# Two experts' maximum as one product with w1 - w2, and Q transposed by the DMA from batch 2 on

## The chip, the cores and the metric

The kernel runs on one core of one Trainium2 chip. The metric is device time in microseconds (us). The engines are named as in the profile: PE is TensorE, PEld its weight loads, DVE is VectorE, ACT is ScalarE, POOL is GpSimd, SP is SyncE. POOL and SP issue the DMAs here.

## What is computed

A linear attention in front of a layer with two experts, of which the larger value is taken element by element:

```python
k_proj = np.einsum('ks,bhsd->bhkd', E, k)          # 8 batches, 8 heads, 1024 tokens, 64 wide
v_proj = np.einsum('ks,bhsd->bhkd', F, v)          # E, F: 64 x 1024
scores = scale * np.matmul(q, k_proj.transpose(0, 1, 3, 2))
attn = softmax(scores)
attn_out = np.matmul(attn, v_proj)
x = attn_out.transpose(0, 2, 1, 3).reshape(8192, 512)
h1 = x @ w1                                        # 512 x 1024
h2 = x @ w2                                        # 512 x 1024
out = np.maximum(h1, h2) @ w_out                   # 1024 x 512
```

Inputs and output are float32; the products are taken in float16 with float32 sums.

## The kernel before

The main loop runs over the 8 batches of 1024 tokens. In it PE works through the expert layer of batch b, and between its blocks stand, one step at a time, the pieces of the attention of batch b + 1. The order is written out by hand: each engine runs its instructions in the order of the program.

`moe_blocks` gives 24 blocks for a batch, in two halves of 512 tokens (j). A half has 8 `up` blocks and then 4 `down` blocks. An `up` block makes 128 of the 1024 hidden columns: four products with w2 into one PSUM bank, four with w1 into another (L272), each 128x512; ACT copies the first bank to SBUF (h2, L279), and DVE takes the maximum of the second bank and that copy, as float16, into `gt` (L280). A `down` block makes the result for 128 tokens: eight products of `gt` with w_out (L288), an ACT copy (L295) and an output DMA on SP's queue (L296). So every block is eight products.

The attention steps of a batch are: `step_kv` (K and V projected with E and F, 16 products, L147), `step_kpt` (K's projection transposed by PE, L161), and for each of four head pairs p: `step_qt` (eight 128x128 transposes of Q on PE, L180, into a float16 PSUM bank; a DVE copy of it into `qt_sb`, L187), `step_sc` (scores, L197; exp on ACT, L205) and `step_da` (denominators and attention, L216; ln and exp(-ln) on ACT, L224 and L225; and, one block later, the product on DVE into `xt_sb`, L228). `xt_sb` is the transposed x that the `up` blocks read. `plan` says after which block each step stands: `step_kv` after block 4, `step_kpt` after 6, the first `step_qt` and `step_sc` after 7 and 8, the last `step_da` after 20.

Batch 0 has no earlier expert work to stand between. Its attention runs first, by itself (the prologue): `step_kv`, `step_kpt`, then for each pair the next pair's `step_qt` and `step_sc` and a `step_da_half` for the first 512 tokens (L242, L250, L251, L254). The second halves stand behind the first four blocks of batch 0.

PSUM has four banks of tag `mm` (products of the expert layer, projections, transposes) and two double banks of tag `att`. Loads go through POOL's queue and turn float32 into float16 on the way; `k_sb`, `v_sb` and `q_sb` have two buffers each, so a load for batch b + 3 waits until batch b + 1 has been read. POOL's order is: K, V, Q of batch 0, the weights in chunks of 256 columns (w2 and w1 in turn), w_out, then K, V, Q of each further batch.

Of the kernel before, what the change touches and what calls it, by code (L numbers as in the profile page):

```python
# [16 lines left out]
def kernel(  # L17
# [27 lines left out]
    const = ctx.enter_context(tc.tile_pool(name="const", bufs=1))  # L45
    kvq = ctx.enter_context(tc.tile_pool(name="kvq", bufs=2))
    proj = ctx.enter_context(tc.tile_pool(name="proj", bufs=2))
    soft = ctx.enter_context(tc.tile_pool(name="soft", bufs=2))
    stage = ctx.enter_context(tc.tile_pool(name="stage", bufs=4))
    xpool = ctx.enter_context(tc.tile_pool(name="xpool", bufs=2))  # L50
    gpool = ctx.enter_context(tc.tile_pool(name="gpool", bufs=2))
    hpool = ctx.enter_context(tc.tile_pool(name="hpool", bufs=3))
    opool = ctx.enter_context(tc.tile_pool(name="opool", bufs=4))
    ps = ctx.enter_context(tc.tile_pool(name="ps", bufs=1, space=bass.MemoryType.PSUM))

    def mm_bank(dtype=FP32):
        return ps.tile(
            [128, 512 if dtype == FP32 else 1024], dtype, tag="mm", bufs=4, name="mm_ps"
        )

    def att_banks():
# [7 lines left out]
            name=nc.get_next_instruction_name(),  # L69
# [24 lines left out]
    tiles = {0: alloc_kvq()}  # L94
# [22 lines left out]
    ident16 = const.tile([128, 128], FP16)  # L117
# [17 lines left out]
    def new_attn(t):  # L135
        t["kp"] = proj.tile([KP, H, D], FP16, tag="kp", name="kp_sb")
        t["vp"] = proj.tile([128, H, D], FP16, tag="vp", name="vp_sb")
        t["kpt"] = proj.tile([128, H, KP], FP16, tag="kpt", name="kpt_sb")
        t["xt"] = xpool.tile([128, NP2, 2, HALF], FP16, tag="xt", name="xt_sb")
        t["qt"] = {}  # L140
        t["ex"] = {}

    def step_kv(t):
# [32 lines left out]
    def step_qt(t, p):  # L176
        qt_ps = mm_bank(FP16)
        for e in range(2):
            for i in range(NI):
                nc.tensor.transpose(  # L180
                    out=qt_ps[:, (e * NI + i) * 128 : (e * NI + i + 1) * 128],
                    in_=t["q"][:, 2 * p + e, 2 * i : 2 * i + 2, :],
                    identity=ident16,
                )
        qt = soft.tile([128, 2, HALF], FP16, tag="qt", name="qt_sb")
        t["qt"][p] = qt
        nc.vector.tensor_copy(out=qt.rearrange("q e n -> q (e n)"), in_=qt_ps)  # L187

    def step_sc(t, p):
        sc_ps = att_banks()
        qt = t["qt"].pop(p)
        for o in range(2):
            for e in range(2):
                pos = D * (o ^ e)
                nc.tensor.matmul(  # L197
                    out=sc_ps[pos : pos + KP, e, :],
                    lhsT=t["kpt"][o * D : (o + 1) * D, 2 * p + e, :],
                    rhs=qt[o * D : (o + 1) * D, e, :],  # L200
                    start=True, stop=True,
                )
        ex = stage.tile([128, 2, HALF], FP16, tag="ex", name="ex_sb")
        t["ex"][p] = ex
        nc.scalar.activation(out=ex, in_=sc_ps, func=ACTF.Exp, scale=scale)  # L205
# [29 lines left out]
    def step_da_half(t, p, o):  # L235
        ex = t["ex"][p]
        da_ps = att_banks()
        for i in range(2):
            for e in range(2):
                r = o ^ e  # L240
                rows = slice(r * KP, (r + 1) * KP)
                nc.tensor.matmul(  # L242
                    out=da_ps[e * D : (e + 1) * D, i, :],
                    lhsT=t["vp"][rows, 2 * p + e, :] if i else ones16[rows, :],
                    rhs=ex[rows, e, :],
                    start=True, stop=True,
                )
        ld = soft.tile([128, HALF], FP32, tag="ldh", name="ldh_sb")
        rec = soft.tile([128, HALF], FP32, tag="rech", name="rech_sb")
        nc.scalar.activation(out=ld, in_=da_ps[:, 0, :], func=ACTF.Ln)  # L250
        nc.scalar.activation(out=rec, in_=ld, func=ACTF.Exp, scale=-1.0)  # L251

        def finish():
            nc.vector.tensor_tensor(  # L254
                out=t["xt"][:, p, o, :], in0=da_ps[:, 1, :], in1=rec, op=ALU.mult
            )

        return finish


    def moe_blocks(b, t):
        xt = t["xt"]
        for j in range(2):
            gt = gpool.tile([128, NFB, HALF], FP16, tag="gt", name="gt_sb")
            for fb in range(NFB):
                def up(fb=fb, j=j, gt=gt):
                    banks = []
                    for w_sb in (w2_sb, w1_sb):
                        h_ps = mm_bank()
                        banks.append(h_ps)  # L270
                        for r in range(NDC):
                            nc.tensor.matmul(  # L272
                                out=h_ps,
                                lhsT=w_sb[:, r, fb * 128 : (fb + 1) * 128],
                                rhs=xt[:, r, j, :],
                                start=(r == 0), stop=(r == NDC - 1),
                            )
                    h2 = hpool.tile([128, HALF], FP32, tag="h2", name="h2_sb")
                    nc.scalar.copy(out=h2, in_=banks[0])  # L279
                    nc.vector.tensor_tensor(  # L280
                        out=gt[:, fb, :], in0=banks[1], in1=h2, op=ALU.max
                    )
                yield up
            for i in range(NI):
                def down(i=i, j=j, gt=gt):
                    op_ps = mm_bank()
                    for fb in range(NFB):
                        nc.tensor.matmul(  # L288
                            out=op_ps,
                            lhsT=gt[:, fb, i * 128 : (i + 1) * 128],  # L290
                            rhs=wo_sb[:, fb, :],
                            start=(fb == 0), stop=(fb == NFB - 1),
                        )
                    o_sb = opool.tile([128, DM], FP32, tag="o", name="o_sb")
                    nc.scalar.copy(out=o_sb, in_=op_ps)  # L295
                    nc.sync.dma_start(  # L296
                        out=out.rearrange("(n p c) m -> n p c m", p=128, c=NC)[
                            b, :, 2 * i + j, :
                        ],
                        in_=o_sb,  # L300
                    )
                yield down


    t = tiles[0]
# [11 lines left out]
    first = {n: (step_da_half, n, 1) for n in range(NP2)}  # L317
    plan = {
        4: [(step_kv,)], 6: [(step_kpt,)], 7: [(step_qt, 0)], 8: [(step_sc, 0)],
        9: [(step_qt, 1)], 11: [(step_da, 0)], 12: [(step_sc, 1)], 13: [(step_qt, 2)],  # L320
        14: [(step_da, 1)], 15: [(step_sc, 2)], 16: [(step_qt, 3)], 17: [(step_da, 2)],
        18: [(step_sc, 3)], 20: [(step_da, 3)],
    }

    for b in range(B):
        nxt = None
        if b + 1 < B:
            nxt = tiles[b + 1] = alloc_kvq()
            for n, src in (("k", k), ("v", v), ("q", q)):
                load(nxt, n, src, b + 1, 0, H)  # L330
            new_attn(nxt)
        pending = None
        for n, block in enumerate(moe_blocks(b, tiles[b])):
            block()
            if pending is not None:
                pending()
                pending = None
            if b == 0 and n in first:
                s = first[n]
                pending = s[0](tiles[0], *s[1:])  # L340
            if nxt is None:
                continue
            for s in plan.get(n, ()):
                r = s[0](nxt, *s[1:])
                if r is not None:
                    pending = r
        del tiles[b]


# [28 lines left out]
```

## Time and profile before

| | us |
|---|---|
| median of 3 runs | 439.12 |
| lowest, highest | 438.16, 440.35 |
| the profiled execution | 439.34 |
| its span, first to last instruction | 437.6 |
| DVE busy, ACT busy in the span | 160.7, 215.4 |

The page gives, for each engine, its busy time as a share of the span; then a chain of work followed back from the last instruction, at each step to whatever released it; and groups of instructions by line, with the mean duration of one. A matmul's duration (382 ns in the group of L272) is longer than the distance from one to the next, since they are pipelined. The granted clock of PE is 1.000 over the span.

```profile
L272 PE MATMUL mm_ps<-xt_sb,w_sb 128*128 128x512 f16 x1024 | 237.2, 382 | 0.7 <-DVE xt_sb L254 0.7
L288 PE MATMUL mm_ps<-wo_sb,gt_sb 128*128 128x512 f16 x512 | 116.7, 379 | 0.0
```

The line of a group reads: line, engine, operation, written <- read, shape, count | busy us in total, mean ns of one | idle us of the engine before them, and what ended it.

### The profile page before, as it was taken

The page shows a single profiled execution, that of the slowest core. Times are in us where ns is not written, and L with a number is a line of the kernel's source. Part 1 is how long each engine was busy: PE and PEld are TensorE (multiplying, and loading weights), DVE is VectorE, ACT ScalarE, POOL GpSimd, SP SyncE. Part 2 cuts the span into 40 slices and gives each one's busy share as a digit, 9 for nine tenths or more (in the row PEclk, how much of TensorE's full clock was granted, in tenths as well). Part 3 has the DMA queues.
Part 4 walks back from the last instruction along what each step waited for, and adds up shares of the span by engine and source line. Part 5 has one row for each costly group of instructions (what it writes and reads, how often), then busy time and mean ns, then how long its engine had stood idle before and what let it go on. Part 6 is the DMA issues. An engine that isn't in the chain of part 4 may idle for free.

```text
span 437.6 us, 5860 instructions
## 1 busy us (share of the span) xinstructions
PE 413.1 (94%) x2352; PEld 180.3 (41%) x2352; DVE 160.7 (37%) x231; ACT 215.4 (49%) x322; POOL 31.8 (7%) x44
## 2 busy tenths in 40 slices
PE   2558999999999999999999999999999999999996
PEld 1232343444444444444443444444443444344442
DVE  0132543524163343524263243524254342434130
ACT  1145547643566346653466345743476336653332
POOL 6450100001000010001000010000000000000000
PEclk9999999999999999999999999999999999999999
DMA  9999999924907195532917177350100102020202
GB/s 163 202 198 207 207 212 242 155 97 61 228 6 140 49 144 145 80 114 29 220 41 128 66 120 170 55 140 1 72 25 25 73 0 97 0 79 19 97 0 96
DMA packets 39707, 45.99 MB, mean 105 GB/s; under 512 B 1664, under 2 KB 31360, under 8 KB 39680
## 3 DMA queue, kind: packets, MB, share of 16 engines
q0 software_dynamic: 30304, 28.31, 41.5%
q1 hardware_dynamic: 9376, 17.31, 10.7%
q8 instruction: 18, 0.29, 0.3%
q14 instruction: 9, 0.07, 0.1%
HBM read 57.15 MB, written 16.78 MB: 169 GB/s over the span
## 4 chain that ended last, share of the span: by engine, by line
PE 92%; DMA 3%; ACT 2%; DVE 1%; issue 1%; POOL 1%; POOLq 0%
PE mm_ps L272 52%; PE mm_ps L288 26%; PE mm_ps L147 4%; PE att_ps L216 4%; PE mm_ps L180 3%; PE att_ps L197 3%; DMA v_sb<-in_v_dram 3%; ACT ex_sb L205 1%; DVE qt_sb L187 1%; PE att_ps L242 1%; ACT rech_sb L251 1%; ACT ldh_sb L250 1%; PE mm_ps L161 0%; POOL k_sb L89 0%; DVE xt_sb L254 0%
## 5 line engine op out<-in xcount | busy, mean ns | idle before, releaser
L272 PE MATMUL mm_ps<-xt_sb,w_sb 128*128 128x512 f16 x1024 | 237.2, 382 | 0.7 <-DVE xt_sb L254 0.7
L280 DVE TENSOR_TENSOR gt_sb<-mm_ps,h_sb 128x512 f16<-128x512 f32 x128 | 88.3, 690 | 174.3 <-PE mm_ps L272 101.8
L272 PEld LDWEIGHTS <-w_sb 128*128 128x128 f16 x1024 | 94.9, 98 | 124.7 <-issue 21.2
L288 PE MATMUL mm_ps<-wo_sb,gt_sb 128*128 128x512 f16 x512 | 116.7, 379 | 0.0
L279 ACT COPY h_sb<-mm_ps 128x512 f32<-128x512 f32 x128 | 74.6, 583 | 79.6 <-PE mm_ps L272 79.6
L295 ACT COPY o_sb<-mm_ps 128x512 f32<-128x512 f32 x64 | 37.4, 584 | 80.6 <-PE mm_ps L288 80.6
L288 PEld LDWEIGHTS <-gt_sb 128*128 128x128 f16 x512 | 48.3, 98 | 58.3 <-issue 4.5
L228 DVE TENSOR_TENSOR xt_sb<-att_ps,rec_sb 128x1024 f16<-128x1024 f32 x28 | 34.1, 1217 | 24.7 <-ACT rec_sb L225 24.7
L205 ACT ACTIVATE ex_sb<-att_ps 128x1024 f16<-128x1024 f32 x32 | 32.9, 1027 | 7.7 <-PE att_ps L197 7.7
L224 ACT ACTIVATE ld_sb<-att_ps 128x1024 f32<-128x1024 f32 x28 | 28.8, 1027 | 8.9 <-PE att_ps L216 8.9
L187 DVE COPY qt_sb<-mm_ps 128x1024 f16<-128x1024 f16 x32 | 21.9, 683 | 25.8 <-PE mm_ps L180 25.7
L225 ACT ACTIVATE rec_sb<-ld_sb 128x1024 f32<-128x1024 f32 x28 | 29.6, 1057 | 0.9
L147 PE MATMUL mm_ps<-k_sb,eft 128*64 128x512 f16 x64 | 17.2, 413 | 6.6 <-DMA k_sb<-in_k_dram 6.6
L180 PEld LDWEIGHTS <-q_sb 128*128 128x128 f16 x256 | 17.9, 103 | 8.8 <-issue 1.2
L180 PE MATMUL mm_ps<-ident,q_sb 128*128 128x128 f16 x256 | 21.2, 230 | 0.0
L197 PE MATMUL att_ps<-qt_sb,kpt_sb 64*64 64x512 f16 x128 | 14.0, 428 | 5.7 <-DVE qt_sb L187 5.7
L147 PE MATMUL mm_ps<-v_sb,eft 128*64 128x512 f16 x64 | 17.0, 413 | 1.9 <-DMA v_sb<-in_v_dram 1.9
L154 ACT CAST kp_sb<-mm_ps 64x512 f16<-64x512 f32 x8 | 4.6, 579 | 26.9 <-PE mm_ps L147 26.9
L89 POOL DMA_DIRECT2D q_sb<-in_q_dram x11 | 9.0, 824 | 121.2 <-PE mm_ps L180 120.7
L89 POOL DMA_DIRECT2D k_sb<-in_k_dram x9 | 7.8, 864 | 116.2 <-PE mm_ps L147 114.2
L155 DVE CAST vp_sb<-mm_ps 64x512 f16<-64x512 f32 x8 | 5.6, 694 | 25.4 <-ACT kp_sb L154 25.4
L147 PEld LDWEIGHTS <-eft 128*64 128x64 f16 x128 | 7.3, 116 | 17.7 <-issue 13.4
(33 smaller groups left out, 101.6 us busy)
## 6 DMA issues: line engine op xcount, KB each, us to landing
out_dram<-o_sb SPq DMA_DIRECT2D x64, 256.0 KB, 2.0
k_sb<-in_k_dram POOLq DMA_DIRECT2D x7, 1024.0 KB, 9.4
v_sb<-in_v_dram POOLq DMA_DIRECT2D x7, 1024.0 KB, 16.6
q_sb<-in_q_dram POOLq DMA_DIRECT2D x7, 1024.0 KB, 9.7
w_sb<-in_moe_w_dram POOLq DMA_DIRECT2D x8, 256.0 KB, 10.4
k_sb<-in_k_dram POOLq DMA_DIRECT2D x2, 512.0 KB, 8.4
v_sb<-in_v_dram POOLq DMA_DIRECT2D x2, 512.0 KB, 10.3
q_sb<-in_q_dram POOLq DMA_DIRECT2D x4, 256.0 KB, 13.3
```

The source lines that it names most:

```text
L147: nc.tensor.matmul(out=kv_ps[i * KP : (i + 1) * KP, :], lhsT=eft[:, i, c, :], rhs=t[n][:, :, c, :], start=(c == 0), stop=(c == NC - 1),)
L180: nc.tensor.transpose(out=qt_ps[:, (e * NI + i) * 128 : (e * NI + i + 1) * 128], in_=t["q"][:, 2 * p + e, 2 * i : 2 * i + 2, :], identity= ...
L197: nc.tensor.matmul(out=sc_ps[pos : pos + KP, e, :], lhsT=t["kpt"][o * D : (o + 1) * D, 2 * p + e, :], rhs=qt[o * D : (o + 1) * D, e, :], s ...
L205: nc.scalar.activation(out=ex, in_=sc_ps, func=ACTF.Exp, scale=scale)
L224: nc.scalar.activation(out=ld, in_=dn_ps, func=ACTF.Ln)
L225: nc.scalar.activation(out=rec, in_=ld, func=ACTF.Exp, scale=-1.0)
L228: nc.vector.tensor_tensor(out=t["xt"][:, p, :, :], in0=at_ps, in1=rec, op=ALU.mult)
L272: nc.tensor.matmul(out=h_ps, lhsT=w_sb[:, r, fb * 128 : (fb + 1) * 128], rhs=xt[:, r, j, :], start=(r == 0), stop=(r == NDC - 1),)
L279: nc.scalar.copy(out=h2, in_=banks[0])
L280: nc.vector.tensor_tensor(out=gt[:, fb, :], in0=banks[1], in1=h2, op=ALU.max)
L288: nc.tensor.matmul(out=op_ps, lhsT=gt[:, fb, i * 128 : (i + 1) * 128], rhs=wo_sb[:, fb, :], start=(fb == 0), stop=(fb == NFB - 1),)
L295: nc.scalar.copy(out=o_sb, in_=op_ps)
```

## The change

Three things are changed together.

1. max(h1, h2) = h2 + relu(h1 - h2). So out = relu(x @ (w1 - w2)) @ w_out + x @ (w2 @ w_out). `wd_sb` = w1 - w2 is formed by DVE in four pieces (`step_wd`), w2 is transposed by PE in four pieces (`step_w2t`), both in the prologue, and `m_sb` = w2 @ w_out is formed by 32 products in front of the first `down` of batch 0 (`step_m`). An `up` is now four products and one DVE instruction; a `down` has twelve products, four of them with `m_sb`.
2. From batch 2 on, Q is transposed by one DMA per batch on SP's queue (`step_qt_dma`), all heads into one tile `qt_sb`, in place of four `step_qt`.
3. The work of a batch is cut into 40 slots of four products (`moe_slots`: 8 `up` slots and four times three `down` slots for each half), and the places of the attention steps are written anew for them (`core`, `by_pe`, `by_dma`).

```diff
-        t["qt"] = {}
...
-        qt = soft.tile([128, 2, HALF], FP16, tag="qt", name="qt_sb")
-        t["qt"][p] = qt
-        nc.vector.tensor_copy(out=qt.rearrange("q e n -> q (e n)"), in_=qt_ps)
+        if "qt" not in t:
+            t["qt"] = qtp.tile([128, H, HALF], FP16, tag="qt", name="qt_sb")
+        nc.vector.tensor_copy(
+            out=t["qt"][:, 2 * p : 2 * p + 2, :].rearrange("q e n -> q (e n)"), in_=qt_ps
+        )
+
+    def step_qt_dma(t):
+        t["qt"] = qtp.tile([128, H, HALF], FP16, tag="qt", name="qt_sb")
+        nc.sync.dma_start_transpose(
+            out=t["qt"].rearrange("q h (i p) -> q (h i) p", p=128),
+            in_=t["q"].rearrange("p h c d -> p (h c d)"),
+        )
...
                 def up(fb=fb, j=j, gt=gt):
-                    banks = []
-                    for w_sb in (w2_sb, w1_sb):
-                        h_ps = mm_bank()
-                        banks.append(h_ps)
-                        for r in range(NDC):
-                            nc.tensor.matmul(
-                                out=h_ps,
-                                lhsT=w_sb[:, r, fb * 128 : (fb + 1) * 128],
-                                rhs=xt[:, r, j, :],
-                                start=(r == 0), stop=(r == NDC - 1),
-                            )
-                    h2 = hpool.tile([128, HALF], FP32, tag="h2", name="h2_sb")
-                    nc.scalar.copy(out=h2, in_=banks[0])
-                    nc.vector.tensor_tensor(
-                        out=gt[:, fb, :], in0=banks[1], in1=h2, op=ALU.max
-                    )
+                    h_ps = mm_bank()
+                    for r in range(NDC):
+                        nc.tensor.matmul(
+                            out=h_ps,
+                            lhsT=wd_sb[:, r, fb * 128 : (fb + 1) * 128],
+                            rhs=xt[:, r, j, :],
+                            start=(r == 0), stop=(r == NDC - 1),
+                        )
+                    nc.vector.tensor_scalar_max(gt[:, fb, :], h_ps, 0.0)
                 yield up
             for i in range(NI):
...
+                for part in range(3):
+                    def down(i=i, j=j, gt=gt, cell=cell, toks=toks, part=part):
+                        if part == 0:
+                            cell["ps"] = mm_bank()
+                        op_ps = cell["ps"]
+                        for n in range(4 * part, 4 * part + 4):
+                            if n < NFB:
+                                lhsT, rhs = gt[:, n, toks], wo_sb[:, n, :]
+                            else:
+                                lhsT, rhs = xt[:, n - NFB, j, toks], m_sb[:, n - NFB, :]
+                            nc.tensor.matmul(
+                                out=op_ps, lhsT=lhsT, rhs=rhs,
+                                start=(n == 0), stop=(n == NFB + NDC - 1),
+                            )
+                        if part < 2:
+                            return
...
+    def step_wd(f0):
+        nc.vector.tensor_tensor(
+            out=wd_sb[:, :, f0 : f0 + 256], in0=w1_sb[:, :, f0 : f0 + 256],
+            in1=w2_sb[:, :, f0 : f0 + 256], op=ALU.subtract,
+        )
+
+    def step_w2t(f0):
+        ps_t = mm_bank(FP16)
+        for f in range(2):
+            for r in range(NDC):
+                nc.tensor.transpose(
+                    out=ps_t[:, (f * NDC + r) * 128 : (f * NDC + r + 1) * 128],
+                    in_=w2_sb[:, r, f0 + f * 128 : f0 + (f + 1) * 128],
+                    identity=ident16,
+                )
+        fb = f0 // 128
+        nc.scalar.copy(
+            out=w2t_sb[:, fb : fb + 2, :].rearrange("q f m -> q (f m)"), in_=ps_t
+        )
+
+    def step_m(r):
+        m_ps = mm_bank()
+        for fb in range(NFB):
+            nc.tensor.matmul(
+                out=m_ps, lhsT=w2t_sb[:, fb, r * 128 : (r + 1) * 128], rhs=wo_sb[:, fb, :],
+                start=(fb == 0), stop=(fb == NFB - 1),
+            )
+        nc.scalar.copy(out=m_sb[:, r, :], in_=m_ps)
...
         step_da_half(t, p, 0)()
+        step_w2t(256 * p)
+        step_wd(256 * p)
...
-        4: [(step_kv,)], 6: [(step_kpt,)], 7: [(step_qt, 0)], 8: [(step_sc, 0)],
...
+        7: (step_kv,), 9: (step_kpt,), 13: (step_sc, 0),
+        17: (step_da, 0), 19: (step_sc, 1), 23: (step_da, 1), 25: (step_sc, 2),
+        29: (step_da, 2), 31: (step_sc, 3), 35: (step_da, 3),
+    }
+    by_pe = {11: (step_qt, 0), 16: (step_qt, 1), 22: (step_qt, 2), 28: (step_qt, 3)}
+    by_dma = {1: (step_qt_dma,)}
...
+            steps = {**core, **(by_dma if b else by_pe)}
...
+            if b == 0 and n == NFB:
+                for r in range(NDC):
+                    step_m(r)
+            slot()
```

In the changed kernel the lines are other ones: the up products are L280, the evictions of `gt` L286, the down products L301, the output copies and DMAs L308 and L309, the DMA transposition L194, scores L206, exp L214, the half steps' product on DVE L263.

How the order moves on the engines is shown at three places. In the rows a number behind a name is a buffer's; `waits` lists the counters that an instruction waits for (DMAHW: a DMA of SP's queue; DMASW: one of POOL's; the others are engines).

On DVE, in the prologue, before the change, from the first copy of transposed Q to the last product of the prologue (`rech_sb` holds the reciprocals of the denominators):

```order
L187 COPY qt_sb_186<-mm_ps_177 128x1024
L187 COPY qt_sb_204<-mm_ps_195 128x1024
L254 TENSOR_TENSOR xt_sb_147<-att_ps_213,rech_sb_219 128x512
L187 COPY qt_sb_232<-mm_ps_223 128x1024
L254 TENSOR_TENSOR xt_sb_147<-att_ps_241,rech_sb_247 128x512
L187 COPY qt_sb_260<-mm_ps_251 128x1024
L254 TENSOR_TENSOR xt_sb_147<-att_ps_269,rech_sb_275 128x512
L254 TENSOR_TENSOR xt_sb_147<-att_ps_279,rech_sb_285 128x512
```

And after it, at the same place:

```order
L187 COPY qt_sb_192<-mm_ps_201 128x1024
L263 TENSOR_TENSOR xt_sb_153<-att_ps_218,rech_sb_224 128x512
L323 TENSOR_TENSOR wd_sb_147<-w1_sb_110,w2_sb_111 128x4x256
L187 COPY qt_sb_192<-mm_ps_239 128x1024
L263 TENSOR_TENSOR xt_sb_153<-att_ps_256,rech_sb_262 128x512
```

A subtraction of a weight chunk now stands between each product and the next copy of Q.

On ACT, in the prologue, after the change, from the exp of the fourth head pair's scores on (`ldh_sb`, `rech_sb` are the ln and the reciprocal):

```order
L214 ACTIVATE ex_sb_292<-att_ps_287 128x1024
L259 ACTIVATE ldh_sb_299<-att_ps_294 128x512
L260 ACTIVATE rech_sb_300<-ldh_sb_299 128x512
L338 COPY w2t_sb_149<-mm_ps_304 128x1024
L259 ACTIVATE ldh_sb_320<-att_ps_315 128x512
L260 ACTIVATE rech_sb_321<-ldh_sb_320 128x512
L338 COPY w2t_sb_149<-mm_ps_325 128x1024
```

The copies of the transposed w2 (L338) are the new rows; before, the second ln stood directly behind the first reciprocal.

On SP, around the start of the loop of batch 1, before the change:

```order
L296 DMA out_0_dram<-o_sb_778 128x512 [waits Activation_49]
L296 DMA out_0_dram<-o_sb_791 128x512 [waits DMAHW0_49,Activation_49]
L296 DMA out_0_dram<-o_sb_803 128x512 [waits DMAHW1_49,Activation_49]
L296 DMA out_0_dram<-o_sb_970 128x512 [waits DMAHW2_49,Activation_49]
L296 DMA out_0_dram<-o_sb_989 128x512 [waits DMAHW3_49,Activation_49]
```

And after it:

```order
L309 DMA out_0_dram<-o_sb_760 128x512 [waits Activation_49]
L309 DMA out_0_dram<-o_sb_790 128x512 [waits DMAHW0_49,Activation_49]
L309 DMA out_0_dram<-o_sb_807 128x512 [waits DMAHW1_49,Activation_49]
L194 DMA_TRANSPOSE qt_sb_833<-q_sb_812 128x32x128 [waits DMASW6_49,DMAHW2_49,DVE_49,PE_49]
L309 DMA out_0_dram<-o_sb_913 128x512 [waits DMAHW3_49,Activation_49]
```

The transposition stands behind the last output of batch 0 and ahead of the first of batch 1; it waits for the load of `q_sb`, and for the earlier readers and writers of its buffer.

More of the change, by code (lines that the diff above doesn't have):

```diff
@@ L48 @@
     soft = ctx.enter_context(tc.tile_pool(name="soft", bufs=2))
+    qtp = ctx.enter_context(tc.tile_pool(name="qtp", bufs=2))
     stage = ctx.enter_context(tc.tile_pool(name="stage", bufs=4))
@@ L184, in step_qt @@
                 )
-        qt = soft.tile([128, 2, HALF], FP16, tag="qt", name="qt_sb")
-        t["qt"][p] = qt
-        nc.vector.tensor_copy(out=qt.rearrange("q e n -> q (e n)"), in_=qt_ps)
+        if "qt" not in t:
[9 more added lines that the diff above has]
+        )
     def step_sc(t, p):
         sc_ps = att_banks()
-        qt = t["qt"].pop(p)
         for o in range(2):
@@ L199, in step_sc @@
                     lhsT=t["kpt"][o * D : (o + 1) * D, 2 * p + e, :],
-                    rhs=qt[o * D : (o + 1) * D, e, :],
+                    rhs=t["qt"][o * D : (o + 1) * D, 2 * p + e, :],
                     start=True, stop=True,
@@ L258, in step_da_half, with moe_slots @@
         return finish
-    def moe_blocks(b, t):
+    def moe_slots(b, t):
         xt = t["xt"]
@@ L283, in moe_blocks @@
+                    nc.vector.tensor_scalar_max(gt[:, fb, :], h_ps, 0.0)
                 yield up
             for i in range(NI):
[L285 to L292, printed above, removed]
-                        )
[L294 to L301, printed above, removed]
@@ L302, in moe_blocks @@
-                yield down
+                cell = {}
+                toks = slice(i * 128, (i + 1) * 128)
+                for part in range(3):
[14 more added lines that the diff above has]
+                            return
+                        o_sb = opool.tile([128, DM], FP32, tag="o", name="o_sb")
+                        nc.scalar.copy(out=o_sb, in_=op_ps)
+                        nc.sync.dma_start(
+                            out=out.rearrange("(n p c) m -> n p c m", p=128, c=NC)[
+                                b, :, 2 * i + j, :
+                            ],
+                            in_=o_sb,
+                        )
+                    yield down
@@ new lines @@
+    wd_sb = const.tile([128, NDC, DF], FP16)
+    m_sb = const.tile([128, NDC, DM], FP16)
+    w2t_sb = const.tile([128, NFB, DM], FP16)
+    def step_wd(f0):
[16 more added lines that the diff above has]
+        )
@@ L315 @@
         step_da_half(t, p, 0)()
-    first = {n: (step_da_half, n, 1) for n in range(NP2)}
-    plan = {
-        4: [(step_kv,)], 6: [(step_kpt,)], 7: [(step_qt, 0)], 8: [(step_sc, 0)],
-        9: [(step_qt, 1)], 11: [(step_da, 0)], 12: [(step_sc, 1)], 13: [(step_qt, 2)],
-        14: [(step_da, 1)], 15: [(step_sc, 2)], 16: [(step_qt, 3)], 17: [(step_da, 2)],
-        18: [(step_sc, 3)], 20: [(step_da, 3)],
-    }
+        step_w2t(256 * p)
+        step_wd(256 * p)
+    core = {
+        7: (step_kv,), 9: (step_kpt,), 13: (step_sc, 0),
+        17: (step_da, 0), 19: (step_sc, 1), 23: (step_da, 1), 25: (step_sc, 2),
+        29: (step_da, 2), 31: (step_sc, 3), 35: (step_da, 3),
+    }
+    by_pe = {11: (step_qt, 0), 16: (step_qt, 1), 22: (step_qt, 2), 28: (step_qt, 3)}
+    by_dma = {1: (step_qt_dma,)}
     for b in range(B):
         nxt = None
+        steps = {}
         if b + 1 < B:
@@ L331 @@
             new_attn(nxt)
+            steps = {**core, **(by_dma if b else by_pe)}
         pending = None
-        for n, block in enumerate(moe_blocks(b, tiles[b])):
-            block()
+        for n, slot in enumerate(moe_slots(b, tiles[b])):
+            if b == 0 and n == NFB:
+                for r in range(NDC):
+                    step_m(r)
+            slot()
             if pending is not None:
@@ L337 @@
                 pending = None
[L338 to L346, printed above, removed]
+            if b == 0 and n % 2 == 0 and n < 2 * NP2:
+                pending = step_da_half(tiles[0], n // 2, 1)
+            if n in steps:
+                s = steps[n]
+                pending = s[0](nxt, *s[1:])
         del tiles[b]
```

## The prediction

> **What bounds the kernel now.** I read the page first, then the chain of waits in order of time, then the groups.
>
> ```profile
> span 437.6 us, 5860 instructions
> PE 413.1 (94%) x2352; PEld 180.3 (41%) x2352; DVE 160.7 (37%) x231; ACT 215.4 (49%) x322; POOL 31.8 (7%) x44
> PE 92%; DMA 3%; ACT 2%; DVE 1%; issue 1%; POOL 1%; POOLq 0%
> ```
>
> PE is busy nearly always, and 92% of the chain that ended last is PE's own work. No other engine reaches half. A share can hide a stage with another limit, so the chain is read in order of time:
>
> ```profile
> 106.58 0.22 PE mm_ps L161 x4
> ...
> 142.47 8.63 PE mm_ps L272 x40
> 151.11 1.85 PE mm_ps L147 x16
> ...
> 161.08 1.83 PE mm_ps L288 x8
> 163.36 3.45 PE mm_ps L288 x16
> 166.81 0.56 PE att_ps L216 x8
> ...
> 192.41 8.63 PE mm_ps L272 x40
> ...
> 392.17 13.81 PE mm_ps L272 x64
> 405.99 6.91 PE mm_ps L288 x32
> ...
> 433.65 0.59 ACT o_sb L295
> ```
>
> Columns are start, length, what. From batch 1 on each piece starts where the last ended: PE never waits. One 128x512 product costs 8.63 / 40 = 0.2158 us, and 13.81 / 64 says the same for the last batch, which has nothing between its products. A loop over one batch takes 192.41 - 142.47 = 49.94 us: 192 products (41.44) and 8.50 us of the next batch's attention. So what the change does to the number of PE instructions goes straight into the time, as long as PE stays the bound.
>
> **Products.** Per batch, before, two up products and one down product: 128 + 64 = 192. After: 64 up with w1 - w2, and 8 row blocks of 12 down (8 of gt, 4 of x with the formed matrix), 96; together 160. Eight batches lose 32 each: 256 x 0.2158 = **-55.2 us**. Forming the matrix (step_m) adds 32 products of the same shape once, in front of slot 8 of batch 0, on PE's path: **+6.9 us**.
>
> **Q transposed by PE.** A step_qt costs PE what it puts between two blocks: from 161.08 to 163.36 are 2.28 us, of which a block of eight is 1.73, so 0.55. Six batches lose four each: 24 x 0.55 = **-13.2 us**. If the next block's pipeline fill came back elsewhere, only the eight transposes' own 0.45 would go (the row of 108.63 below): -10.8. Nothing else on PE changes from batch 1 on, so a loop should come to 49.94 - 6.91 - 2.20 = 40.83 us.
>
> **Prologue.** Here PE does not bind. The chain before the first full product:
>
> ```profile
> 23.67 0.98 PE mm_ps L180 x8
> ...
> 33.17 0.69 DVE qt_sb L187
> 33.90 0.67 PE att_ps L197 x4
> 34.59 0.86 ACT ex_sb L205
> 35.52 0.60 ACT ldh_sb L250
> 36.14 0.63 ACT rech_sb L251
> 36.77 0.61 ACT ldh_sb L250
> 37.40 0.64 ACT rech_sb L251
> 38.06 0.70 DVE xt_sb L254
> 38.80 2.29 PE mm_ps L272 x5
> ...
> 108.63 0.45 PE mm_ps L180 x8
> ```
>
> ```profile
> L280 DVE TENSOR_TENSOR gt_sb<-mm_ps,h_sb 128x512 f16<-128x512 f32 x128 | 88.3, 690 | 174.3 <-PE mm_ps L272 101.8
> L228 DVE TENSOR_TENSOR xt_sb<-att_ps,rec_sb 128x1024 f16<-128x1024 f32 x28 | 34.1, 1217 | 24.7 <-ACT rec_sb L225 24.7
> L205 ACT ACTIVATE ex_sb<-att_ps 128x1024 f16<-128x1024 f32 x32 | 32.9, 1027 | 7.7 <-PE att_ps L197 7.7
> L187 DVE COPY qt_sb<-mm_ps 128x1024 f16<-128x1024 f16 x32 | 21.9, 683 | 25.8 <-PE mm_ps L180 25.7
> ```
>
> It goes round once per head pair: qt copy, scores, exp, ln, exp, product, next qt copy. On DVE a step_wd now stands between the product and the next qt copy. Of the four, those of pairs 0 and 1 delay a qt copy; that of pair 2 has over 2 us until the last product (a w2t copy, ln and exp of ACT are ahead of it), that of pair 3 is behind it. No row shows a subtraction of f16 in SBUF: 0.68 us is the copy of as many f16 elements (L187), 1.22 the product of as many from f32 (L228). I take the copy, both sides being f16: 2 x 0.68 = 1.4, at most 2.4; below nothing it cannot go. On ACT the w2t copies (128x1024 f16 from PSUM, 1.03 by L205) of pairs 0 and 1 lie beside DVE's product, wd and qt copy (over 2 us); that of pair 2 stands on the chain, between the reciprocal of pair 2 and the ln of pair 3: +1.0. Their 32 transposes on PE (0.98 per eight at this point) fit in PE's gaps, ahead of the ACT copies that read them. Together **+2.4 us** (2.1 to 3.5).
>
> PE also runs at half speed here: the same eight transposes took 0.98 us at 23.67 and 0.45 at 108.63, and the first products cost 2.29 / 5 = 0.46. I leave that cost as it is. The Trainium skill ("TensorE: Matmul & The Clock Gate", What's actually happening) says that the clock doubles after about 3.4 us of sustained PE work. The trace agrees that the half speed ends only once products run densely. By that rule the added transposes might warm PE before the first product, and the sum would be up to 2.2 us (an estimate: ten products at 0.22 saved) lower.
>
> **Weights in time.** step_wd, step_w2t and step_m need weights earlier than now.
>
> ```profile
> 22.71 0.89 POOL L113 DMA_DIRECT2D wo_sb<-in_moe_w_out_dram  x1 [0.59 <-DMA w_sb<-in_moe_w_dram]
> ```
>
> ```profile
> wo_sb<-in_moe_w_out_dram POOLq DMA_DIRECT2D x1, 1024.0 KB, 14.8
> ```
>
> w_out is the last weight issued: it lands at 22.71 + 14.8 = 37.5. step_m comes after the first half's eight up products, past 50. The last w1 chunk is issued before it and is read only by wd of pair 3, past 41. No wait: nothing.
>
> **Q transposed by the DMA.** Nothing in the trace does this. What it must meet: step_qt_dma is issued behind the last output of the batch before, so after an o_sb copy of 0.59 and an issue of SP's, some 1.2 us into the loop. The first reader is step_sc of pair 0 after slot 13: 14 groups of four products (12.1), step_kv (1.85 and 0.1 of fill) and step_kpt (0.22) earlier, or 14.2 us into the loop. So 13.0 us are free. It reads q_sb, loaded over a loop earlier, and no output is due on SP before slot 10.
>
> ```profile
> 0.74 0.57 SPq L79 DMA_DIRECT2D ef_sb<-in_E_dram  x1
> ```
>
> ```profile
> q0 software_dynamic: 30304, 28.31, 41.5%
> q1 hardware_dynamic: 9376, 17.31, 10.7%
> ...
> out_dram<-o_sb SPq DMA_DIRECT2D x64, 256.0 KB, 2.0
> k_sb<-in_k_dram POOLq DMA_DIRECT2D x7, 1024.0 KB, 9.4
> ```
>
> Bounds for its 1 MB: four times the 256 KB output's 2.0 us is 8; the same bytes into the same shape take the k load 9.4. If it moves 256 bytes at a time, it is 4096 packets, 256 on each of 16 engines; a packet costs 0.107 x 16 x 437.6 / 9376 = 0.080 us on q1 and 0.096 on q0, so 20.5 to 24.5 us. I take the k load's 9.4: the same bytes, and packet times there hold larger packets. Landed at 10.6 of 14.2: **hidden, nothing**, with 3.6 us to spare. The loads of a later batch, which share the engines, start only when step_kv has read its k, at about 8 us.
>
> The Trainium skill ("VectorE: DVE Perf Modes", The three transpose paths) speaks against this edit: 1309 ns for a 128x128 block by the DMA, 390 by TensorE. In series its 32 blocks would be 41.9 us, and the sum 6 x 28.9 higher, about 554 (an estimate); no run here shows it yet, and the trace's PE does a block in 0.45 / 8 = 0.06.
>
> **What lies beside.** In the up stage each slot is 0.863 us of PE and one eviction of DVE. The new form (a maximum with 0) has no row; L280 reads the same PSUM tile at 0.69, and I take that. It becomes the bound above 0.863. ACT loses 128 copies that nothing waited for: no gain. At the hand-over to the next batch, PE does four slots after step_da of pair 3 and three products more before it reads the last xt: 3.45 + 0.65 = 4.1 us. The trace needs 89.36 + 1.23 - 87.25 = 3.3:
>
> ```profile
> 86.86 0.39 PE L216 MATMUL att_ps<-ex_sb,vp_sb 64*64 64x512 f16 x4
> ...
> 89.36 1.23 DVE L228 TENSOR_TENSOR xt_sb<-att_ps,rec_sb 128x1024 f16<-128x1024 f32 x1 [3.53 <-ACT rec_sb L225]
> ```
>
> **Sum**, on the profiled execution's 439.34 us (span 437.6; the median of the runs is 439.12, the same within 0.1%): 439.34 - 55.2 + 6.9 - 13.2 + 2.4 = **380.2**, said as 380. With the bounds above (qt +2.4, prologue -0.3 to +1.1, clock -2.2) 378 to 384, and with small waits at the new joints up to 386.
>
> **Rivals.**
> DVE late in the second up stage: eight evictions and one 1.22 us product (5.5 + 1.2 = 6.7) must fit in eight slots and the attention between them (6.9 + 0.56 + 0.34 = 7.8), and the product stands waiting for ACT in the middle. The second third of the first down block reads the eighth gt 1.5 us after its last product. For: the slack is about a quarter microsecond. Against: DVE is 37% busy. If it costs 1 us in each of seven loops: 387.
> The transposition partly late, 13.0 to 22.9 us: each microsecond over 13.0 costs six. For: the packet bound of 20.5, which gives 7.5 x 6 = 45, or 425. Against: the k load at 9.4.
> Slower than before: the transposition over 22.9 us. The gain of 59.1 is eaten when six scores wait 59.1 / 6 = 9.9 us each, at slot 13. At 24.5 it is 11.7 each, or 450. For: q0's packet time. Against: packets of a quarter of the bytes or less should not cost as much as whole ones. Its far end, 0.01 of the chance, is a transposition that takes its 32 blocks one after another at the latency of the output's DMA: 32 x 2.0 = 64 us, 51 exposed, 686. The Trainium skill's block figure above is this mechanism at its own price.
> The first product starting warm is inside the range.
>
> **Chances.** Forecast 0.77, DVE late 0.07, partly late 0.10, slower 0.06. The range 377 to 390 holds the forecast, the DVE case and the first microsecond or so of the partly late case: 0.85. The two late cases are left out, though the packet bounds reach into them, since they hold 0.15. A measurement of this kernel tells about 0.5% from no change: faster by more 0.94, within 0.01, slower 0.05 (a little of the slow case ends inside 0.5%).
>
> **What would show it.** The chain of waits from batch 1 on: L280 and L301 pieces without a gap, 40.8 us from loop to loop, 34.5 in the last. L206 waiting for qt_sb from the DMA: the transposition is late, and its time from issue to landing says by how much. PE waiting for DVE at L301: the DVE case. The first product that waits for xt_sb at about 41.2 instead of 38.80: the prologue. The prediction is wrong if a scores step waits on SP's queue, or if a product's pitch is no longer 0.216.

## The result and the profile after

| | before | after |
|---|---|---|
| median of the runs, us | 439.71 | 381.18 |
| lowest, highest | 438.16, 440.35 | 380.06, 381.38 |
| the profiled execution | 439.34 | 380.06 |
| its span | 437.6 | 378.3 |

The ratio is 0.8668 with a 95% interval of 0.8638 to 0.8699: 13% faster. The prediction said 380. One of the six runs of `reorder`, below, took 426.07 us at a granted clock of 0.863 and does not enter its ratio, though it does enter its median (378.26 us without it). These are the first lines of the page and of its chain of waits, as shown of the kernel before:

```profile
span 378.3 us, 4743 instructions
PE 353.2 (93%) x1968; PEld 149.3 (39%) x1968; DVE 149.8 (40%) x211; ACT 152.0 (40%) x202; POOL 31.8 (8%) x44
PE 90%; DMA 3%; ACT 3%; DVE 2%; issue 1%; POOL 1%; ACTq 0%; POOLq 0%
```

PE is still the bound, with 384 fewer matmul instructions. The chain of waits of the changed kernel in order of time (start, length, what):

```profile
40.55 0.38 PE mm_ps L280
...
92.62 6.91 PE mm_ps L280 x32
...
103.43 3.56 PE mm_ps L301 x16
106.99 0.34 PE att_ps L206 x4
...
133.87 6.91 PE mm_ps L280 x32
...
340.10 6.91 PE mm_ps L280 x32
...
364.27 10.37 PE mm_ps L301 x48
374.71 0.59 ACT o_sb L308
```

From batch 1 on there is no gap, as before. A product still takes 6.91 / 32 = 0.216 us. A loop takes 133.87 - 92.62 = 41.25 us where it took 49.94, the last batch 34.55 where it took 41.45. Scores (L206) follow the products without a wait, so the transposed Q is there in time. Its rows, from the DMA issues and from SP's timeline:

```profile
qt_sb<-q_sb SPq DMA_TRANSPOSE x6, 5.7
```

```profile
93.27 0.33 SPq L309 DMA_DIRECT2D out_dram<-o_sb  x1
93.78 4.11 SPq L194 DMA_TRANSPOSE qt_sb<-q_sb  x1
```

It is issued 1.16 us into the loop of batch 1 and holds SP's queue for 4.1 us. The median from issue to landing is 5.7 us (the first one took 7.2). The scores come at 106.99, 13.2 us after issue.

The evictions of the up products on DVE, from the groups:

```profile
L286 DVE TENSOR_SCALAR gt_sb<-mm_ps 128x512 f16<-128x512 f32 x128 | 87.1, 689 | 40.5 <-PE mm_ps L280 40.5
```

### The profile page after: what moved, and what is told of

Same layout as the page of the kernel before. It is cut to its first block, busy times and chain, and to the rows that moved or that the text cites. A ratio compares the mean times of both kernels' runs of the same rounds, so it can differ in the third digit from the quotient of the medians.

```text
span 378.3 us, 4743 instructions
## 1 busy us (share of the span) xinstructions
PE 353.2 (93%) x1968; PEld 149.3 (39%) x1968; DVE 149.8 (40%) x211; ACT 152.0 (40%) x202; POOL 31.8 (8%) x44
## 3 DMA queue, kind: packets, MB, share of 16 engines
q1 hardware_dynamic: 34144, 23.60, 20.2%
## 4 chain that ended last, share of the span: by engine, by line
PE 90%; DMA 3%; ACT 3%; DVE 2%; issue 1%; POOL 1%; ACTq 0%; POOLq 0%
PE mm_ps L301 45%; PE mm_ps L280 30%; PE mm_ps L147 4%; PE att_ps L225 4%; DMA v_sb<-in_v_dram 3%; PE att_ps L206 3%; PE mm_ps L345 2%; ACT ex_sb L214 1%; PE mm_ps L180 1%; DVE qt_sb L187 1%; ACT rech_sb L260 1%; ACT ldh_sb L259 1%; PE att_ps L251 1%; PE mm_ps L161 0%; DVE wd_sb L323 0%
## 5 line engine op out<-in xcount | busy, mean ns | idle before, releaser
L301 PE MATMUL mm_ps<-wo_sb,gt_sb 128*128 128x512 f16 x512 | 123.8, 380 | 0.0
L280 PE MATMUL mm_ps<-xt_sb,wd_sb 128*128 128x512 f16 x512 | 116.6, 380 | 0.8 <-DVE xt_sb L263 0.8
L286 DVE TENSOR_SCALAR gt_sb<-mm_ps 128x512 f16<-128x512 f32 x128 | 87.1, 689 | 40.5 <-PE mm_ps L280 40.5
L280 PEld LDWEIGHTS <-wd_sb 128*128 128x128 f16 x512 | 47.9, 98 | 61.8 <-issue 7.7
L301 PEld LDWEIGHTS <-gt_sb 128*128 128x128 f16 x512 | 47.8, 98 | 61.9 <-issue 8.5
L301 PE MATMUL mm_ps<-m_sb,xt_sb 128*128 128x512 f16 x256 | 65.9, 380 | 0.0
L308 ACT COPY o_sb<-mm_ps 128x512 f32<-128x512 f32 x64 | 37.3, 582 | 69.9 <-PE mm_ps L301 60.5
L214 ACT ACTIVATE ex_sb<-att_ps 128x1024 f16<-128x1024 f32 x32 | 32.9, 1027 | 8.6 <-PE att_ps L206 8.6
L301 PEld LDWEIGHTS <-xt_sb 128*128 128x128 f16 x256 | 23.3, 98 | 31.4 <-issue 5.8
L206 PE MATMUL att_ps<-qt_sb,kpt_sb 64*64 64x512 f16 x128 | 13.6, 414 | 6.5 <-DVE qt_sb L187 6.5
L225 PE MATMUL att_ps<-ex_sb,ones 64*64 64x512 f16 x112 | 11.5, 400 | 0.0
L206 PEld LDWEIGHTS <-kpt_sb 64*64 64x64 f16 x128 | 3.9, 104 | 19.0 <-issue 13.6
## 6 DMA issues: line engine op xcount, KB each, us to landing
q_sb<-in_q_dram POOLq DMA_DIRECT2D x4, 256.0 KB, 13.5
```

What stands on the lines that cost most here:

```text
L206: nc.tensor.matmul(out=sc_ps[pos : pos + KP, e, :], lhsT=t["kpt"][o * D : (o + 1) * D, 2 * p + e, :], rhs=t["qt"][o * D : (o + 1) * D, 2 * ...
L225: nc.tensor.matmul(out=dst[e * D : (e + 1) * D, o, :], lhsT=ones16[rows, :] if w is None else w[rows, 2 * p + e, :], rhs=ex[rows, e, :], s ...
L280: nc.tensor.matmul(out=h_ps, lhsT=wd_sb[:, r, fb * 128 : (fb + 1) * 128], rhs=xt[:, r, j, :], start=(r == 0), stop=(r == NDC - 1),)
L286: nc.vector.tensor_scalar_max(gt[:, fb, :], h_ps, 0.0)
L301: nc.tensor.matmul(out=op_ps, lhsT=lhsT, rhs=rhs, start=(n == 0), stop=(n == NFB + NDC - 1),)
```

## The experiments

The theory: PE binds from batch 1 on, so the gain is what was taken off PE; the DMA transposition is free only because it lands before its reader and before the next loads start. The rivals: the transposition has a hidden price of its own, or its place does not matter. Two sizes differ from the forecast and have to be explained: loops take 41.25 us instead of 40.83, and the start is faster.

### Each half of the change by itself

`q_by_pe`: the changed kernel, with all Q transposed by PE.

```diff
-            steps = {**core, **(by_dma if b else by_pe)}
+            steps = {**core, **by_pe}
```

> The changed kernel with Q transposed by PE in all batches (the four step_qt at slots 11, 16, 22, 28 in every loop), all else kept. Theory A (the DMA transposition is hidden, and a step_qt costs PE only its eight transposes, 0.45 us, because the 0.10 us of fill stays with the block): six loops get 4 x 0.45 longer, 41.25 to 43.05 us, 381.2 + 10.8 = 392.0 us. Theory B (0.55 per step, as the prediction took): loops of 43.45, 394.4 us. Theory C (the DMA transposition costs PE something that the chain does not show, by contention): less than 10.8 longer, below 391.

Measured: 391.02 us, ratio to before 0.8922 (0.8891 to 0.8953). The chain of waits from loop to loop:

```profile
92.50 6.91 PE mm_ps L280 x32
...
135.53 6.91 PE mm_ps L280 x32
...
146.34 1.83 PE mm_ps L301 x8
148.17 0.45 PE mm_ps L180 x8
148.62 1.73 PE mm_ps L301 x8
```

The loop is 135.53 - 92.50 = 43.03 us, 1.78 longer than with the DMA: 0.45 for each of four steps. That is Theory A; the time alone, 1 us below A's 392.0, would not have kept it from Theory C. The row before the transposes has 1.83 for eight products, the one behind them 1.73. The 0.10 us more belongs to the block behind a step whose matmuls use only part of the array (64*64, 128*64 or 64*128 in the rows; here `step_kpt`), and no such 0.10 follows the transposes of Q, which use all of it. The loop is also 49.94 - 43.03 = 6.91 us shorter than before, exactly the 32 products, so the new slots by themselves neither gain nor cost anything per loop.

`dma_q_alone`: the kernel before, with the DMA transposition only (`step_qt_dma` and the one tile `qt_sb` as in the change; shown is where it is issued).

```diff
...
+            if b and n == 0:
+                step_qt_dma(nxt)
             for s in plan.get(n, ()):
+                if b and s[0] is step_qt:
+                    continue
                 r = s[0](nxt, *s[1:])
```

> The kernel before, with only the DMA transposition of Q from batch 2 on, issued after block 0; both expert products stay. Theory A: loops of 49.94 - 1.80 = 48.14 us, 439.7 - 10.8 = 428.9 us. Theory B (0.55 per step): loops of 47.74, 426.5 us. If the gain of the transposition needed the new slots: 439 us or more.

Measured: 427.09 us, ratio 0.9735 (0.9693 to 0.9776), which is 11.6 us of 439.21 with an interval of 9.8 to 13.5.

```profile
92.16 8.63 PE mm_ps L280 x40
...
140.31 8.63 PE mm_ps L280 x40
```

The loop is 48.15 us, 1.79 shorter than before: Theory A by the loop, while the time alone fits both theories. The transposition does not need the new slots. The two halves add up: as shares of the time before, 10.8% (all but the DMA) and 2.65% make 13.4%, and both together gave 13.3%.

### The place of the transposition

`dma_q_late`: the changed kernel with the transposition issued behind slot 10.

```diff
-    by_dma = {1: (step_qt_dma,)}
+    by_dma = {10: (step_qt_dma,)}
```

> The changed kernel with the DMA transposition issued after slot 10 in place of slot 1. It then starts some 0.7 us after slot 10, and PE reaches the scores 2.7 us after it. Theory A (it lands 5.7 us after issue, as at slot 1, loads beside it or not): PE waits 3.7 us in each of six loops, 381.2 + 22 = 403 us. Theory B (it slows down beside the K, V and Q loads that step_kv has just let start, at least to twice its time): 6 us or more of wait per loop, 417 us or more. Theory C (its place does not matter): 381 us.

Measured: 461.9 us, ratio 1.0528 (1.0495 to 1.0561): slower than the kernel before. All the gain of the change and 23 us more are gone through one number. The chain of waits, and POOL's and PE's timelines of this run:

```profile
104.78 2.13 PE mm_ps L301 x10
106.91 16.34 DMA qt_sb<-q_sb
123.38 0.64 PE att_ps L206 x3
124.02 5.25 PE mm_ps L301 x16
```

```profile
103.02 0.88 POOL L90 DMA_DIRECT2D k_sb<-in_k_dram  x1 [19.13 <-PE mm_ps L147]
103.89 0.88 POOL L90 DMA_DIRECT2D v_sb<-in_v_dram  x1
```

```profile
123.38 0.64 PE L206 MATMUL att_ps<-qt_sb,kpt_sb 64*64 64x512 f16 x4 [15.04 <-DMA qt_sb<-q_sb]
...
345.16 0.41 PE L206 MATMUL att_ps<-qt_sb,kpt_sb 64*64 64x512 f16 x4 [4.25 <-DMA qt_sb<-q_sb]
```

step_kv has just let the K and V loads of a later batch start (103.02 and 103.89), and the transposition beside them lands after 16.3 us. The control stands in the same run: the loops of batches 5 and 6 have nothing left to load, and there the transposition lands after 5.6 us. PE waits 15 us four times and 4 twice. So the loads triple it: Theory B, which had named 6 us of wait as the least. Theory A's wait, 3.7, is close to the 4.25 of the two loops without loads. A wait also costs what follows it, which neither theory counted: after 15.04 us of idling the next 16 products took 5.25 us instead of 3.56, the first of them at half speed.

`reorder_dma1`, below, moves batch 1's transposition into the loop of batch 0 in the same manner.

### The prologue

`before_warm`: the kernel before, with the 32 transposes of w2 added in the prologue. Nothing reads what they write.

```diff
+    def warm(f0):
+        ps_t = mm_bank(FP16)
+        for f in range(2):
+            for r in range(NDC):
+                nc.tensor.transpose(
+                    out=ps_t[:, (f * NDC + r) * 128 : (f * NDC + r + 1) * 128],
+                    in_=w2_sb[:, r, f0 + f * 128 : f0 + (f + 1) * 128],
+                    identity=ident16,
+                )
...
         step_da_half(t, p, 0)()
+        warm(256 * p)
```

> The kernel before, with the four times eight transposes of w2 added in the prologue behind step_da_half; nothing reads what they write. Theory A (the added PE work takes PE out of half speed before the first product): scores in the prologue take 0.44 instead of 0.67, batch 0's loop is about 1.7 us shorter and starts about 0.5 earlier, about 437.4 us. Theory B (half speed ends at a time of its own): no change of the loop, 439.7 to 441 us.

Measured: 437.92 us, ratio 0.9978 (0.9960 to 0.9995). Work was added, and the time fell by about 1 us, a change that the interval only just tells from none. PE's timeline of this run:

```profile
26.21 0.64 PE L197 MATMUL att_ps<-qt_sb,kpt_sb 64*64 64x512 f16 x4 [0.78 <-DVE qt_sb L187]
...
30.45 0.41 PE L197 MATMUL att_ps<-qt_sb,kpt_sb 64*64 64x512 f16 x4 [0.95 <-DVE qt_sb L187]
...
37.69 2.83 PE L272 MATMUL mm_ps<-xt_sb,w_sb 128*128 128x512 f16 x8
...
41.00 1.90 PE L272 MATMUL mm_ps<-xt_sb,w_sb 128*128 128x512 f16 x8
```

The third scores step is at full speed (0.41 for 0.64). The first eight products are slow again, the next eight are not. Batch 1 starts at 91.36 where it started at 92.53, although the prologue began 0.8 us later in this run (step_kpt at 21.15 for 20.36). That is Theory A, with part of its gain lost when PE fell back.

The other traces bear it out, with one limit. In the three prologues without these transposes (before, `dma_q_alone`, `w2t_late`) the eight products behind the first half step are still partly slow, 2.06 to 2.68 us; in the seven with them they take 1.90. But where in the prologue full speed returns differs from trace to trace: at the third scores step here, in the changed kernel and in `evict_twice`, at the fourth in `q_by_pe` and `reorder`, while in `dma_q_late` and `reorder_dma1` the fourth still takes 0.64, although `dma_q_late` has the changed kernel's prologue.

`w2t_late`: the changed kernel with those transposes moved in front of step_m.

```diff
-        step_w2t(256 * p)
...
+                for p in range(NP2):
+                    step_w2t(256 * p)
                 for r in range(NDC):
                     step_m(r)
```

> The changed kernel with the four step_w2t moved out of the prologue, directly in front of step_m. Theory A (the transposes in the prologue are what warmed PE): the 32 transposes cost 1.8 to 2.2 on PE's path, the ACT copy leaves the chain (-0.7), and the half speed at the start of batch 0 comes back (+1.7, and +0.5 in the prologue): about 384.6 us. Theory B (the clock has nothing to do with them): 381.2 + 2.0 - 0.7 = 382.5 us. The batch 0 loop in the trace tells them apart.

Measured: 385.02 us, ratio 0.8758 (0.8731 to 0.8785), 4.5 us more span than the changed kernel. Lines of its PE timeline and of its chain:

```profile
40.51 0.59 PE L280 MATMUL mm_ps<-xt_sb,wd_sb 128*128 128x512 f16 x1 [0.68 <-DVE xt_sb L263]
...
42.02 2.68 PE L280 MATMUL mm_ps<-xt_sb,wd_sb 128*128 128x512 f16 x8
```

```profile
50.98 1.89 PE mm_ps L147 x16
...
53.47 3.71 ACT w2t_sb L338 x4
57.23 5.79 PE mm_ps L345 x26
```

The time fits Theory A, but not for its reasons alone. Half speed is back at the first products (2.68 for 1.90), and from 40.51 to step_kv at 50.98 are 10.47 us where the changed kernel needs 9.04: 1.4 us. The other 3.1 us come from the edit: PE waits for the four ACT copies, which now stand in a row in front of step_m. I had not counted that wait. So the run shows that the half speed returns, and its total shows nothing about it.

`reorder`: the changed kernel with step_wd of pairs 0 and 1 behind a copy of Q, and the w2t copy of pair 2 behind the last reciprocal. step_w2t now returns its ACT copy, to be called later.

```diff
             step_qt(t, p + 1)
+            if p < 2:
+                step_wd(256 * p)
             step_sc(t, p + 1)
-        step_da_half(t, p, 0)()
-        step_w2t(256 * p)
-        step_wd(256 * p)
+        finish = step_da_half(t, p, 0)
+        if p != 3:
+            finish()
+        copy = step_w2t(256 * p)
+        if p < 2:
+            copy()
+        elif p == 2:
+            late = copy
+            step_wd(512)
+        else:
+            finish()
+            late()
+            copy()
+            step_wd(768)
```

> The changed kernel with the prologue's order mended: step_wd of pairs 0 and 1 directly behind a copy of Q, where DVE waits for ACT anyway, and the w2t copy of pair 2 behind the last reciprocal. Theory A (two subtractions, 2 x 0.61, and one ACT copy, 0.66, stand on the prologue's chain): the last product of the prologue starts 1.9 us earlier, 381.2 - 1.9 = 379.3 us. Theory B (PE, at half speed, or a weight chunk that has not landed takes their place): 381 us.

Measured: 378.46 us, ratio to before 0.8612 (0.8587 to 0.8636). That is the fastest version, and its interval lies just below that of the changed kernel (0.8638 to 0.8699). PE's timeline:

```profile
38.07 0.38 PE L280 MATMUL mm_ps<-xt_sb,wd_sb 128*128 128x512 f16 x1 [0.82 <-DVE xt_sb L263]
```

The last product of the prologue is 2.5 us earlier than in the changed kernel (40.55). The prologue of this run also began some 0.6 us earlier (the second scores step at 24.98 instead of 25.61), so 1.9 us are the edit: Theory A. One trace each does not fix that size: from the second scores step to the last product are 13.09 us here, but 14.00 in `reorder_dma1`, which has the same prologue with its third and fourth scores at half speed; the changed kernel has 14.94.

`reorder_dma1`: as `reorder`, with batch 1's Q transposed by the DMA too.

```diff
-            steps = {**core, **(by_dma if b else by_pe)}
+            steps = {**core, **by_dma}
```

> As the run named reorder, and batch 1's Q is transposed by the DMA too (slot 1 of batch 0). Theory A (it lands before slot 13 there too): another 4 x 0.45 = 1.8 us less, 377.5 us. Theory B (the loads keep the DMA engines full until past 60 us, the transposition waits for q_sb until about 58 and then takes at least twice its 5.7 us): PE waits up to 5 us at the scores of slot 13, 379 to 383 us.

Measured: 401.36 us, ratio 0.9129 (0.9101 to 0.9158), 23 us more than `reorder`. SP's and PE's timelines:

```profile
52.50 20.95 SPq L194 DMA_TRANSPOSE qt_sb<-q_sb  x1
```

```profile
84.08 0.64 PE L206 MATMUL att_ps<-qt_sb,kpt_sb 64*64 64x512 f16 x4 [21.11 <-DMA qt_sb<-q_sb]
```

Theory B, with its size far too small: among the loads at the start of the kernel the transposition took 31.5 us from issue to landing instead of 5.7, and PE waited 21.1. It also held SP's queue for 21 us, with the outputs behind it.

### DVE as the next bound

`evict_twice`: each eviction of `gt` is done twice.

```diff
                     nc.vector.tensor_scalar_max(gt[:, fb, :], h_ps, 0.0)
+                    nc.vector.tensor_scalar_max(gt[:, fb, :], h_ps, 0.0)
```

> The changed kernel with each eviction of gt done twice by DVE, same result. DVE then needs 2 x 0.61 us per up slot of 0.863. Theory A (DVE is the next bound of the up stage, with about a quarter us of slack at the first down block): about 2 us of PE waits per loop and 4 in the last, 396 to 406 us. Theory B (DVE has room, the four PSUM banks cover it): below 384 us.

Measured: 429.75 us from one execution, 49 more. In the chain of waits (L287 is the second eviction) DVE takes the place of PE in the up stage:

```profile
142.85 0.88 PE mm_ps L280 x4
143.75 0.70 DVE gt_sb L286
144.47 0.69 DVE gt_sb L287
...
145.80 0.69 DVE gt_sb L287
...
190.52 0.88 PE mm_ps L280 x4
```

The direction is Theory A's; the size is not. A pair takes 145.80 - 144.47 = 1.33 us, not 1.22: the second eviction starts 0.72 us after the first, when that has ended, and the next pair 0.61 after the second. That the 0.72 comes from writing the same bytes is my reading; no run separates it. The four PSUM banks hide less of it than I thought: a loop grows by 190.52 - 142.85 - 41.25 = 6.4 us, not 2. With one eviction a slot leaves 0.863 - 0.69 = 0.17 us of DVE's time free, or 0.25 by the 0.61 from one pair to the next.

## Why the prediction was right, step by step

**Products: right.** Each loop lost the 32 products' 6.91 us and the four transpositions. The last loop, which has no attention in it, went from 41.45 to 34.55. The pitch stayed at 0.216.

**Forming the matrix: right.** step_m took 7.01 us on PE's path, with w_out there in time (expected 6.9):

```profile
51.44 7.01 PE mm_ps L345 x32
```

**A step_qt's price: mis-sized.** The prediction took 0.55 from 2.28 - 1.73 and named 0.45 as the other end. The block in that subtraction stood behind a scores step and so had 1.83 itself; 2.28 - 1.83 is 0.45. `q_by_pe` shows it. This term was 10.8 us, not 13.2, and it makes the loops 0.42 longer than forecast, 2.5 us in six.

**Prologue: mis-sized, the other way.** The mechanism was right: the subtractions and one w2t copy stand on the chain.

```profile
29.11 0.68 DVE wd_sb L323
29.79 0.61 DVE qt_sb L187
...
37.08 0.63 ACT rech_sb L260
37.71 0.66 ACT w2t_sb L338
38.51 0.61 ACT ldh_sb L259
```

The last product came at 40.55, 1.75 later than before, not 2.4. Two subtractions delay what is behind them by 0.61 each (forecast 0.68), and the w2t copy delays the ln by 38.51 - 37.71 = 0.80 (forecast 1.0). Two things have nothing to do with these terms: two scores steps ran at full speed (0.44 and 0.45 for 0.67), which saved 0.45 and does not happen in every execution, as `dma_q_late` shows; and this execution's prologue was 0.19 later from the start (second scores step at 25.61 for 25.42). 1.22 + 0.80 - 0.45 + 0.19 gives about 1.75.

**Half speed at the start: left as it was, and it changed.** From that product to batch 1 the changed kernel takes 92.62 - 40.55 = 52.07 us, the one before 53.73. For those 1.66 us the prediction's range had left room, up to 2.2, by the rule of the Trainium skill ("TensorE: Matmul & The Clock Gate", What's actually happening) that sustained PE work ends the slow clock. `before_warm` and the first products of `w2t_late` agree with that direction; no run here measures the 3.4 us. The errors nearly cancel: +2.5 in the loops, against -0.65 and -1.66 at the start and about -0.3 behind the last product (437.6 - 433.6 before, 378.3 - 374.6 after). That the total fits to a few tenths is luck; its terms do not.

**The DMA transposition hidden: right.** It landed after 5.7 us in the median, below the 9.4 that the prediction took and below its lower bound of 4 x 2.0. The packet price behind the upper bound (20.5 to 24.5 us) is refuted: queue q1 has 34144 packets on the changed kernel's page where it had 9376, about 4100 more for each transposition, as that bound assumed, and they landed in a quarter of its time. Such times do come, 16.3 and 31.5, but from loads beside it. Here the prediction was also lucky. It knew that the next loads start about 8 us into the loop, took 10.6 for the landing, and gave the stretch in which both would run no price; `dma_q_late` shows that it has one. What keeps the change on the good side is that the transposition is faster than forecast, and its place. POOL's timeline of the changed kernel has the next load here:

```profile
101.67 0.87 POOL L90 DMA_DIRECT2D k_sb<-in_k_dram  x1 [19.13 <-PE mm_ps L147]
```

Issued at 93.78, the transposition has landed by 101.0 in this loop (7.2 us), 0.7 us ahead of that load, and usually after 5.7. A kernel slower than before has been seen, in `dma_q_late`, but through loads beside a later transposition, not through a price of its own as in the prediction's rival. The block figure of the Trainium skill ("VectorE: DVE Perf Modes", The three transpose paths), 1309 ns, would be 41.9 us for 32 blocks in series; measured without loads beside it, it is 5.7 / 32 = 0.18 us a block, so they do not go in series at that price, and the measurement decides.

**DVE: right, with little room.** The chain has no DVE piece from batch 1 on, at 0.69 us of each 0.863.

## What to carry to other kernels

On an engine without gaps a cut is worth the instructions' own pitch; subtract like from like, since a block behind one step can cost more than the same block behind another. A transfer that replaces work on the bound engine was free here only in a window without loads: find out what lets the next loads start, and issue it long enough before that. Preparing weights once costs little when it stands where its engine waits anyway; when several engines take turns in a chain, each added piece belongs behind the instruction after which that engine is idle.

## What the runs showed of the hardware that was not expected

- A transposition of 1 MB by the DMA took 5.6 to 5.7 us without loads beside it (6.1 and 7.2 once each in the changed kernel), 16.3 us beside two loads of 1 MB, and 31.5 us among the loads at the start. It held SP's queue for about 4.1, 14.3 and 21.0 us of that.
- PE falls back to half speed soon: after a wait of 4.25 us in `dma_q_late` eight products took 3.27 us instead of 1.89, although the scores directly behind the wait still ran at full speed (0.41).

```profile
345.50 3.27 PE L301 MATMUL mm_ps<-wo_sb,gt_sb 128*128 128x512 f16 x8
```

- The granted clock of the profile does not show the half speed reliably. Over the same 18 us of the prologue (20 to 38 us; the fields are PE, PEld, DVE, ACT and POOL busy, then the clock, the DMA's share, which can pass 1, and GB/s) the windows give 1.00 for the kernel before, whose transposes took twice their time there, and 0.93 for the changed one:

```profile
20.00:38.00 18.00, 11.71 (x71) 5.58 (x72) 6.54 (x11) 9.68 (x15) 7.62 (x9) 1.00 1.37 200
```

```profile
20.00:38.00 18.00, 10.92 (x92) 6.54 (x92) 7.31 (x13) 10.76 (x16) 7.61 (x9) 0.93 1.37 201
```
